# Token columns riding in the head sums of a backward chain, and key/value gradients moved into a weave

## The chip, the cores and the metric

The kernel runs on one core of one Trainium2 chip. The metric is the device time of one execution in microseconds (us). A span is the time from the first to the last instruction of a profiled execution. An instruction's place in the source is given as L and its line in the kernel before.

## What is computed

Forward and backward pass of a gated mix of two attention layers over 2048 tokens of 576 features, `g * a + (1 - g) * b`. Layer A is multi-query attention with 32 heads of 18. Layer B is attention with a recurrent memory; it is what the change is about:

```
for s in range(64):                                   # segments of 32 tokens
    h = concat([mem, x[32*s : 32*s + 32]])            # 8 memory rows, then 32 token rows
    q, k, v = (h @ W for W in (Wq, Wk, Wv))           # 32 heads of 128
    p = softmax(mask(q @ k.T * scale))                # token rows causal, memory columns free
    o = (p @ v) @ Wo
    mem, out[s] = o[:8], o[8:]
```

The outputs are the result and the gradients of all inputs and weights. The memory rows of a segment depend on those of the one before; in the backward pass their gradient runs through the 64 segments from last to first. All else of layer B can be done for many segments at once.

## The kernel before

**Stages.** They follow each other on the core: `prep` and `a_weights` (transposed copies of the inputs), `make_WoT`, `b_proj` (dense projections), the forward weave, `b_bulk` (token attention of layer B, forward and backward, but for some sums), the backward weave, `b_post` (the last token stage), `b_dw` (weight gradients) and `a_final`. From `make_WoT` to `b_post` instructions stand on each engine in the order in which the program writes them; every engine and every DMA queue works in that order and waits where an operand or a buffer isn't ready.

**A weave** (`weave`) is two generators that take turns: after each step of a chain (to its `yield`) comes one step of a sweep. The sweep is layer A's attention: `a_pass1` forward, `a_pass2` backward, 1024 pairs each. A step of `a_pass2` writes two 128 x 512 score tiles (`b_S`, one buffer), takes their exponential on ACT (`b_E`, L1652), makes two `b_dP` tiles, multiplies on DVE (`b_dS`, L1673) and adds four `b_acc` matmuls of the pair before. QD and SD (`b_QD`, `b_SD`) are loaded every fourth pair, two loads ahead. The chain has 16 steps for each of the 64 segments. In the backward weave the sweep gets 12 steps of lead and twice 10 extra ones at the start, in which `load_WT` brings the weights.

**The backward chain** (`b_chain_bwd`), by its steps: 1 to 3 project the memory's gradient (`dm`, 8 of 32 columns) to the heads (`proj_part`, L264); 4 transposes it (`mem_T`); 5 makes the score gradients `dS` of the memory rows and spreads them to blocks on POOL (`dSB`); 6, 7 and 8 make the gradients of v, q and k (`mem_grad`, for wi = 2, 0, 1), which ACT copies to `dT`, 256 columns for each wi: 8 groups u of 4 heads x 8 rows. `heads` multiplies them with the weights `WT`: for each half of the 576 features, wi and u, four matmuls side by side, one for each group of 8 heads g, each with all 32 columns of the group u on its 32 columns of the array. Of the 32 x 288 results of such a matmul a quarter is used, the head whose weights it has. `sums` picks it: matmuls in f32 with the selection matrix `selF`. `put_rows` (L272) writes the next `dm`. A segment's loads (`load`) are issued in step 8 on SP's queue, 14 and one transpose; small stores go through POOL's queue.

**The fifth slice.** 576 features are four slices of 128 and one of 64. The transposed inputs hold six slots (`NSL`): the fifth slice stands in two, one with its lower and one with its upper 64 rows zero, so that a matmul of it has 128 rows and takes the weights of one of two column halves that share 128 partitions (`W...t`). This holds in `b_proj`, in `b_chain_fwd` and in `b_chain_bwd` by `proj_part`.

**The forward chain** (`b_chain_fwd`) does the same for the memory rows; since its projections have 32 columns and only 8 memory rows, 24 token columns ride along (`put_ride`), and its `heads` (L384 on) multiply each head by itself, 32 x 4 matmuls of 144 columns.

**The last token stage** (`b_post`) has 16 token tiles with 8 groups of 4 heads, 128 group steps, pipelined over three stages: `st_KV` (L1100) adds to the gradients of k and v of the tile's tokens what comes from the tokens' own score gradients (loaded `y_ds`, `y_p`, `y_q`, `y_dO`) and what comes from the memory rows of its four segments (`y_sB` with the block-diagonal `y_qB` and `y_dOB`, cleared once on POOL at L1063); `st_T` transposes them on PE; `st_H` (L1129) multiplies dq, dk and dv with `WT` to the input's gradient, 24 matmuls of 288 columns (`y_pdx`), which goes to `dxB_dram`. dk and dv go to DRAM for `b_dw`.

Of the kernel before, what the change touches and what calls it, by code (L numbers as in the profile page):

```python
# [31 lines left out]
NSL = 6  # L32
# [8 lines left out]
class Kern:  # L41
# [52 lines left out]
    def setup_B_dram(self, dram):  # L94
        T, NSEG, NM, NTT = self.T, self.NSEG, self.NM, self.NTT
        t = lambda nm, sh, dt=BF16: dram.tile(sh, dt, name=nm)
        self.xT_dram = t("xT_dram", [NSL, P, T])
        self.dbT_dram = t("dbT_dram", [NSL, P, T])
# [6 lines left out]
        self.xtok = {w: t(w + "x_dram", [T, J]) for w in ("q", "k", "v", "o", "dO", "dq", "dk", "dv")}  # L105
# [9 lines left out]
        self.pq_dram = t("pq_dram", [NTT, 4, 8, 4, 16, P])  # L115
# [7 lines left out]
    def setup_B_consts(self, pool):  # L123
# [37 lines left out]
        sf = pool.tile([P, 8], F32, name="selF")  # L161
        nc.gpsimd.memset(sf[:], 0.0)
        for c in range(4):
            nc.gpsimd.affine_select(out=sn[:, c, :], in_=sn[:, c, :], compare_op=ALU.not_equal, fill=1.0,
                                    base=-32 * c, pattern=[[-1, 8]], channel_multiplier=1)
            nc.gpsimd.affine_select(out=sf[:], in_=sf[:], compare_op=ALU.not_equal, fill=1.0,
                                    base=-40 * c, pattern=[[-1, 8]], channel_multiplier=1)
        self.seln = sn
        self.selF = sf
# [10 lines left out]
        hm = pool.tile([P, 2, 8], BF16, name="halfmask")  # L180
        nc.gpsimd.memset(hm[:], 0.0)
        for j in range(2):
            nc.gpsimd.memset(hm[64 * j:64 * j + 64, j, :], 1.0)
        self.halfmask = hm
# [27 lines left out]
    def proj_load(self, items, n, sp):  # L212
        if n < len(items) and items[n] not in self.px:
            w, tt = items[n]
            t = sp.tile([P, NSL, P], BF16, name="p_x", bufs=4)
            src = self.dbT_dram if w == "dO" else self.xT_dram
            self.nc.sync.dma_start(t[:], src[:, :, tt * P:(tt + 1) * P].rearrange("k p t -> p k t"))
            for v in ("k", "v", "q") if w != "dO" else (w,):
                self.px[v, tt] = t
# [3 lines left out]
    def b_proj(self, items, n0, n1, sp, psum, extra):  # L223
        nc = self.nc
        due = []
        for n in range(n0, n1):
# [9 lines left out]
            for jc in range(8):  # L236
                pb = psum.tile([P, 512], F32, name="p_pb", bufs=8)
                for kt in range(4):
                    self.mm(pb[:], lhsT=xt[:, kt, :], rhs=Wt[0][:, kt, jc * 512:(jc + 1) * 512],
                            start=(kt == 0), stop=False)  # L240
                self.mm(pb[:], lhsT=xt[:, 4 + jc % 2, :], rhs=Wt[1][:, jc // 2, :], start=False, stop=True)
                self.evac(tok[:, jc * 512:(jc + 1) * 512], pb[:], use="vs"[jc % 2])
# [21 lines left out]
    def proj_part(self, pj, st, Wt, j, kts):  # L264
        for kt in kts:
            for c in range(4):
                lhsT, rhs = ((st[:, kt, :], Wt[0][:, kt, c * 1024 + j * 512:c * 1024 + (j + 1) * 512]) if kt < 4
                             else (st[:, 4 + j, :], Wt[1][:, c, :]))
                self.mm(pj[32 * c:32 * c + 32, :], lhsT=lhsT, rhs=rhs,
                        start=(kt == 0), stop=(kt == NKT - 1), tp=(0, 32 * c))  # L270

    def put_rows(self, t, pm):  # L272
        nc = self.nc
        nc.vector.tensor_copy(t[:, 0:4, 0:8], pm[:, 0:4, :])
        nc.vector.tensor_tensor(out=t[:, 4:6, 0:8], in0=pm[:, 4:5, :].to_broadcast([P, 2, 8]), in1=self.halfmask[:],
                                op=ALU.mult)
# [7 lines left out]
    def b_chain_fwd(self, keep, sp, psum):  # L284
        nc = self.nc
        NSEG = self.NSEG
        hm = [keep.tile([P, NSL, 32], BF16, name=f"hm{i}") for i in range(2)]
# [5 lines left out]
        for kt in range(NKT):  # L293
            for p0, n, r0 in d_rows(kt):
                for j in range(1 if kt < 4 else 2):
                    q0 = p0 + 64 * j
                    nc.gpsimd.dma_start(hm[0][q0:q0 + n, kt + j, 0:8], self.B_mem0[:, r0:r0 + n].rearrange("m d -> d m"))
# [7 lines left out]
        def load_stage(m):  # L305
            t0 = ride(4 * m)[0]
            n = min(96, self.T - t0)
            if n > 0:
                stage[m] = sp.tile([P, NSL, 96], BF16, name="c_rt", bufs=1)
# [9 lines left out]
        put_ride(0)  # L319
        nc.gpsimd.dma_start(self.otok_dram[:, D:NKT * P].rearrange("(n p) d -> p n d", p=P),  # L320
# [31 lines left out]
        for s in range(NSEG):  # L352
# [38 lines left out]
            if s:  # L391
                pm = psum.tile([P, NKT, 8], F32, name="c_pj", bufs=1)
                self.mm(pm[:, 0:4, :].rearrange("p k q -> p (k q)"), lhsT=hs[:],
                        rhs=self.seln[:].rearrange("p c q -> p (c q)"))
                for j in range(2):
                    self.mm(pm[64 * j:64 * j + 64, 4, :], lhsT=hx[:].rearrange("p g c -> p (g c)"), rhs=self.sel8[:],
                            tp=(0, 64 * j))
                self.put_rows(h_, pm)
            yield
            nc.gpsimd.tensor_copy(hist[:, :, s, :], h_[:, 0:NKT, 0:8])  # L400
# [8 lines left out]
            if s % 4 == 0:  # L409
                nc.gpsimd.dma_start(self.pq_dram[s // 4].rearrange("s q c w k -> (s q c) (w k)")  # L410
# [157 lines left out]
    def make_WoT(self, pool, psum):  # L568
        self.alloc_WoT(pool)
        W, Wt = self.WoT  # L570
        for kt in range(4):
            for hg in range(8):
                ptr = psum.tile([P, 640], BF16, name="w_ptr", bufs=4)
                for hl in range(4):
                    h = hg * 4 + hl
                    self.tr(ptr[:, hl * E:(hl + 1) * E], self.WoN[:, h, kt * P:kt * P + P], P)
                self.evac(W[:, kt, hg * 512:(hg + 1) * 512], ptr[:, 0:512])
            self.nc.sync.dma_start(self.st_WoT[kt], W[:, kt, :])
        for c in range(4):
            ptr = psum.tile([P, 640], BF16, name="w_ptr", bufs=4)  # L580
            for j in range(2):
                for hl in range(4):
                    h = 8 * c + 4 * j + hl
                    self.tr(ptr[64 * j:64 * j + 64, hl * E:(hl + 1) * E], self.WoN[:, h, 4 * P:D], P, tp=(0, 64 * j))
# [297 lines left out]
    def b_chain_bwd(self, keep, sp, psum):  # L882
        nc = self.nc
        NSEG = self.NSEG
        dm = [keep.tile([P, NSL, 32], BF16, name=f"dm{i}") for i in range(2)]
        self.load_WoT(keep)
        mrow = {w: keep.tile([P, 8, n * E], BF16, name=f"r_{w}") for w, n in (("q", 1), ("k", 1), ("dx", 2))}
        pads = {w: keep.tile([P, n, 8, 32], BF16, name=f"r_{w}pad") for w, n in (("p", 1), ("ds", 1), ("x", 2))}
        for t in dm + list(mrow.values()) + list(pads.values()):
# [3 lines left out]
        seln = f(self.seln[:])  # L893

        def load(s):
            L = {}
            L["vmT"] = sp.tile([P, HB, 8], BF16, name="r_vmT", bufs=2)
            nc.sync.dma_start(L["vmT"][:], self.mTd["v"][s])
            L["vxT"] = sp.tile([P, HB, 32], BF16, name="r_vxT", bufs=2)
# [3 lines left out]
            L["oT"] = sp.tile([P, 256], BF16, name="r_oT", bufs=2)  # L903
            nc.sync.dma_start(L["oT"][:], self.oTm_dram[s // 16][:, s % 16, :])
            L["kx"] = sp.tile([P, 8, E], BF16, name="r_kx", bufs=2)
            for c in range(4):
                nc.sync.dma_start(L["kx"][32 * c:32 * c + 32].rearrange("p u e -> p (u e)"),
                                  self.xtok["k"][s * 32:(s + 1) * 32, c * 1024:(c + 1) * 1024])
                nc.sync.dma_start(mrow["dx"][32 * c:32 * c + 8],
                                  self.dmx_dram[s * 8:s * 8 + 8, 8 * c:8 * c + 8].rearrange("m h w e -> m h (w e)"))  # L910
# [3 lines left out]

        def to_q(srcs, nm, eng):
            pad = pads[nm]
            for i, src in enumerate(srcs):
                eng.tensor_copy(pad[:, i, :, 0:8], u8(src))
# [9 lines left out]

        nxt = load(NSEG - 1)
        PqB = p_blocks(nxt["pT"])  # L930
        for s in reversed(range(NSEG)):
# [3 lines left out]
            nc.gpsimd.dma_start(self.dmT_dram[:, :, s, :], d_[:, 0:NKT, 0:8])  # L935
# [16 lines left out]
            for c in range(4):  # L952
                nc.gpsimd.dma_start(self.mtok["dO"][s * 8:(s + 1) * 8, c * 1024:(c + 1) * 1024], self.m_rows(dOm, c))
            yield
# [10 lines left out]
            for rg in range(2):  # L965
                for c in range(4):
                    self.mm(pd[32 * c:32 * c + 32, rg, :], lhsT=self.negones[:, 0:32], rhs=prod[:, :, c, :],
                            start=False, stop=True, tp=(0, 32 * c))
            dS = sp.tile([P, 2, 64], BF16, name="r_dS", bufs=1)
# [4 lines left out]
            dT = sp.tile([P, 3, 8, 32], BF16, name="r_dT", bufs=1)  # L974
            hs = sp.tile([P, D], F32, name="r_hs", bufs=1)
            ph = {}

            units = iter([(wi, hf, u) for hf in range(2) for wi in (2, 0, 1) for u in range(8)])

            def heads(n):  # L980
                for _ in range(n):
                    wi, hf, u = next(units)
                    if hf not in ph:
                        ph[hf] = psum.tile([P, 288], F32, name="r_pj", bufs=1)
                    for g in range(4):
                        self.mm(ph[hf][32 * g:32 * g + 32, :], lhsT=dT[:, wi, u, :],
                                rhs=self.WT[wi][:, 8 * g + u, 288 * hf:288 * hf + 288],
# [946 lines left out]
```

## Time and profile before

| | us |
|---|---|
| median of 3 runs | 6115.3 |
| the runs | 6114.51, 6115.3, 6123.61 |
| the profiled execution | 6121.41 |
| its span | 6119.6 |

| engine | busy us | share of the span |
|---|---|---|
| PE | 5639.4 | 92% |
| DVE | 3758.4 | 61% |
| ACT | 3423.1 | 56% |
| POOL | 2163.7 | 35% |

PE is TensorE's matmuls, PEld its weight loads, DVE VectorE, ACT ScalarE, POOL GpSimd, SP the engine that only issues DMAs; SPq is its queue. A line of the timeline has the start in us from the span's start, the time in us from the first of merged instructions to the end of the last, engine, line, operation, `out<-in`, the stationary operand's rows and columns joined by `*`, the moving operand's partitions and elements, and a count; in brackets stands the idle time before it and what ended it. Matmuls are pipelined: the time of a single one (0.39 for 512 columns) is longer than what it adds to a row of them (0.215), so the distance between two starts tells what work costs. L76 and L81 are the helpers that issue all matmuls and most transposes, so that they are told by the names of their tiles.

### The profile page before, as it was taken

How to read it: one execution, taken by the hardware profiler on the slowest of the kernel's cores; microseconds unless marked ns; L12 is line 12 of the kernel's file. 1: busy time of each engine (PE TensorE's matmuls, PEld its weight loads, DVE VectorE, ACT ScalarE, POOL GpSimd, SP SyncE). 2: the span in 40 equal slices, each digit the busy share in tenths (PEclk: the TensorE clock that was granted, in tenths of full speed). 3: DMA queues.
4: the chain of work that ended last, by engine and by line, in shares of the span. 5: the costliest groups of instructions: out<-in, count | busy, mean ns of one | idle time of the engine just before them, and what ended most of it. 6: DMA issues, size and time to landing. Idle time of an engine off the chain costs nothing.

```text
span 6119.6 us, 211593 instructions
## 1 busy us (share of the span) xinstructions
PE 5639.4 (92%) x90477; PEld 3286.1 (54%) x90477; DVE 3758.4 (61%) x7114; ACT 3423.1 (56%) x4842; POOL 2163.7 (35%) x3896
## 2 busy tenths in 40 slices
PE   6899999999999979998879999999998999899999
PEld 4443444444444438777535555555554777675444
DVE  4326888888888866666668888888886111111112
ACT  3325788788787866555557777777775222111101
POOL 4003555545555544444323333333333111112213
PEclk9999999999999989999889999999999999999999
DMA  4644665656565459999853434444443999896663
GB/s 152 221 157 134 134 139 133 139 138 140 133 138 114 107 143 251 252 243 249 246 144 109 108 108 109 109 108 110 109 109 96 239 250 249 236 274 202 209 187 113
DMA packets 1117299, 1000.59 MB, mean 164 GB/s; under 512 B 687353, under 2 KB 942722, under 8 KB 1106722
## 3 DMA queue, kind: packets, MB, share of 16 engines
q1 hardware_dynamic: 1009090, 724.23, 46.0%
q0 software_dynamic: 107264, 262.81, 14.4%
q8 instruction: 709, 11.62, 0.8%
q14 instruction: 236, 1.93, 0.1%
HBM read 551.36 MB, written 386.08 MB: 153 GB/s over the span
## 4 chain that ended last, share of the span: by engine, by line
PE 62%; ACT 14%; DMA 7%; issue 2%; SPq 2%; POOL 1%; DVE 0%; POOLq 0%; DVEq 0%; ACTq 0%
ACT b_E L1652 11%; PE w_acc L76 10%; PE a_acc L76 7%; PE b_S L76 6%; PE c_pj L76 5%; PE y_pdx L76 5%; PE a_S L76 5%; PE r_pj L76 4%; PE c_x L76 3%; DMA dsx_dram<-x_dS 3%; ACT a_E L1515 3%; PE r_x L76 3%; PE x_tr L81 2%; PE b_acc L76 2%; PE y_pk L76 2%
## 5 line engine op out<-in xcount | busy, mean ns | idle before, releaser
L1543 DVE TENSOR_TENSOR a_W<-a_dP,a_E 128x512 bf16<-128x512 f32 x2048 | 1313.0, 685 | 281.7 <-ACT c_k L73 60.6
L1673 DVE TENSOR_TENSOR b_dS<-b_dP,b_E 128x512 bf16<-128x512 f32 x2048 | 1312.9, 682 | 254.0 <-issue 132.8
L1652 ACT ACTIVATE b_E<-b_S 128x1024 bf16<-128x1024 f32 x1024 | 1048.8, 1024 | 423.3 <-PE b_dP L76 326.1
L1515 ACT ACTIVATE a_E<-a_S 128x1024 bf16<-128x1024 f32 x1024 | 1049.2, 1025 | 290.0 <-PE a_dP L76 278.9
L76 PE MATMUL b_S<-b_KV,b_QD 32*128 32x512 bf16 x2048 | 405.9, 386 | 161.4 <-ACT b_E L1652 116.4
L76 PE MATMUL r_pj<-WT,r_dT 128*32 128x288 bf16 x12288 | 494.6, 289 | 1.1 <-ACT r_hs L990 1.1
L76 PE MATMUL w_acc<-w_d,w_h 128*128 128x512 bf16 (+1 forms) x2400 | 473.8, 379 | 0.0
L76 PE MATMUL a_S<-a_QD,l_KV 32*128 32x512 bf16 x2048 | 399.3, 383 | 33.3 <-ACT a_E L1515 18.7
L76 PE MATMUL a_acc<-a_W,l_WK 128*32 128x512 bf16 x4096 | 429.2, 390 | 0.3 <-DVE a_W L1543 0.2
L76 PE MATMUL b_acc<-b_dS,b_SD 128*32 128x512 bf16 x2048 | 423.8, 395 | 0.6 <-DMA b_SD<-sd_dram 0.4
L76 PE MATMUL a_acc<-a_E,l_VK 128*32 128x512 bf16 x4096 | 415.1, 381 | 5.6 <-issue 1.1
L76 PE MATMUL b_acc<-b_E,b_SD 128*32 128x512 bf16 x2048 | 408.8, 396 | 0.0
L76 PE MATMUL a_dP<-a_QD,l_KV 32*128 32x512 bf16 x2048 | 407.3, 385 | 0.0
L76 PE MATMUL b_dP<-b_KV,b_QD 32*128 32x512 bf16 x2048 | 403.9, 391 | 0.0
L1125 DVE COPY y_T<-y_pt 128x512 bf16<-128x512 bf16 x256 | 96.9, 419 | 460.9 <-PE y_pt L81 442.8
L76 PEld LDWEIGHTS <-r_dT 128*32 128x32 bf16 x12288 | 334.6, 97 | 80.0 <-issue 2.3
L76 PEld LDWEIGHTS <-w_h 128*128 128x128 bf16 (+1 forms) x2688 | 229.8, 100 | 258.4 <-issue 6.6
L76 PEld LDWEIGHTS <-b_QD 32*128 32x128 bf16 x4096 | 166.5, 91 | 357.5 <-issue 313.2
L76 PEld LDWEIGHTS <-hm 128*32 128x32 bf16 x7680 | 195.9, 97 | 207.2 <-POOL hm L316 10.7
L1111 ACT CAST y_tdk<-y_pk 128x512 bf16<-128x512 f32 x128 | 75.1, 587 | 380.1 <-PE y_pk L76 214.8
L76 PE MATMUL y_pdx<-WT,y_T 128*128 128x288 bf16 x2048 | 272.9, 287 | 0.0
L725 POOL TENSOR_TENSOR x_P<-x_E,x_r 128x512 bf16<-128x512 bf16 x128 | 133.3, 1041 | 388.3 <-DVE x_r L722 298.2
(444 smaller groups left out, 11603.2 us busy)
## 6 DMA issues: line engine op xcount, KB each, us to landing
b_QD<-qd_dram SPq DMA_DIRECT2D x256, 128.0 KB
b_SD<-sd_dram SPq DMA_DIRECT2D x256, 128.0 KB
dOx_dram<-p_tok SPq DMA_DIRECT2D x16, 1024.0 KB
c_vx<-vx_dram SPq DMA_DIRECT2D x256, 64.0 KB
krow_dram<-c_k POOLq DMA_DIRECT2D x64, 256.0 KB, 2.9
qrow_dram<-c_q POOLq DMA_DIRECT2D x64, 256.0 KB, 3.9
vrow_dram<-c_v POOLq DMA_DIRECT2D x64, 256.0 KB, 3.3
x_q<-qx_dram SPq DMA_DIRECT2D x32, 512.0 KB
```

Of the source, the lines that this page charges most:

```text
L76: return self.nc.tensor.matmul(out, lhsT, rhs, start=start, stop=stop, tile_position=tp, skip_group_check=True)
L81: return self.nc.tensor.transpose(out, in_, self.identB[b:b + nrows, b:b + nrows], tile_position=tp)
L725: nc.gpsimd.tensor_tensor(out=o[:, r, :], in0=Et[:, :, lo:lo + n], in1=rl[:].unsqueeze(2).to_broadcast([P, 4, n]), op=ALU.mult)
L1111: nc.scalar.copy(d[w][:, r, :], pk[:])
L1125: nc.vector.tensor_copy(T_[t][w][:], pt[:])
L1515: nc.scalar.activation(E_[n][:], S.pop(n)[:], ACT.Exp, scale=SCALEA)
L1543: nc.vector.tensor_tensor(out=W_[n][:, i, :], in0=dP[i][:], in1=E_[n][:, i, :], op=ALU.mult)
L1652: nc.scalar.activation(E_[n][:], S.pop(n)[:], ACT.Exp, scale=SCALEA)
L1673: nc.vector.tensor_tensor(out=D_[n][:, i, :], in0=dP[i][:], in1=E_[n][:, i, :], op=ALU.mult)
```

## The change

1. **Riding columns.** `dT` is one kept tile with 32 columns for each of the 32 heads and three gradients. Columns 24 to 31 are the memory rows, which ACT writes as before (and POOL copies to `dTc` for the store); columns 0 to 23 are 24 tokens' dq, dk and dv, which three DMA transposes a segment (`load_dT`) bring from DRAM for 55 of the 64 segments: the last 1320 tokens. `heads` has 96 units instead of 48, each one head and gradient, with four matmuls of 144 columns that cover the 576 features; nothing of a result is thrown away. Two DVE copies, one bf16 matmul and two small ones (`row_sums`, as in the forward chain) take the place of the f32 sums, and the sums' rows 0 to 23 go to `dxr_dram`, from which four DRAM copies in the last stage fill the rows of `dxB_dram`.
2. **Key and value gradients in the weave.** `st_KV`'s work for tiles 15 down to 5 is done in the backward chain, 176 units of four heads and one of dk and dv, four a segment in 44 segments: `kv_mm` in steps 4, 10, 13 and 16, `kv_out` (an ACT copy and a store on POOL, with one buffer) in steps 5, 11, 14 and 16. The memory rows' part is four matmuls of 32 rows instead of one block-diagonal one of 128.
3. **The last stage** has 6 tiles, tokens 0 to 767, and the 32-row form of the sums as well; the block-diagonal buffers and their clearing go.
4. **The fifth slice** has one slot: its matmuls have 64 rows, at row 0 or 64 of the array. `put_rows` is one copy. The columns of `db` and of Wo's transpose are permuted to groups of 144, with four small POOL copies in `make_WoT` and 16 in `prep`.
5. **Buffers.** Several of the chain's loads have one buffer instead of two; `b_KV` is loaded in four parts with two buffers.

The core of the diff:

```diff
@@ proj_part
-                lhsT, rhs = ((st[:, kt, :], Wt[0][:, kt, c * 1024 + j * 512:c * 1024 + (j + 1) * 512]) if kt < 4
-                             else (st[:, 4 + j, :], Wt[1][:, c, :]))
+                r = slice(64 * j, 64 * j + 64)
+                lhsT, rhs, r0 = ((st[:, kt, :], Wt[0][:, kt, c * 1024 + j * 512:c * 1024 + (j + 1) * 512], 0) if kt < 4
+                                 else (st[r, 4, :], Wt[1][r, c, :], 64 * j))
                 self.mm(pj[32 * c:32 * c + 32, :], lhsT=lhsT, rhs=rhs,
-                        start=(kt == 0), stop=(kt == NKT - 1), tp=(0, 32 * c))
+                        start=(kt == 0), stop=(kt == NKT - 1), tp=(r0, 32 * c))
+
+    def row_sums(self, pm, hs, hx, sel, sel8):
+        self.mm(pm[:, 0:4, :].rearrange("p k q -> p (k q)"), lhsT=hs[:, 0:P], rhs=sel[:].rearrange("p c q -> p (c q)"))
+        for j in range(2):
+            self.mm(pm[64 * j:64 * j + 64, 4, :], lhsT=hx[:].rearrange("p g c -> p (g c)"), rhs=sel8[:], tp=(0, 64 * j))
@@ b_chain_bwd
+        def load_dT(s, wi):
+            if 0 <= s < NSEG - KR:
+                t0 = T - RIDE * (NSEG - KR - s)
+                nc.sync.dma_start_transpose(dT[:, wi], self.xtok[("dq", "dk", "dv")[wi]][t0:t0 + 32, :])
...
+        def kv_load(n):
...
+            if w == 0:
+                nc.sync.dma_start(kvS[rg].rearrange("p x i k -> p (x i k)"),
+                                  self.pq_dram[tt, g // 2].rearrange("s q h x i k -> (s q) h (x i k)")[:, g % 2, :])
+                for j, x in enumerate(("dO", "q")):
+                    nc.sync.dma_start(kvR[rg, j].rearrange("p i e -> p (i e)"),
+                                      self.mtok[x][tt * 32:tt * 32 + 32, 512 * g:512 * g + 512])
+            a = sp.tile([P, 4, P], BF16, name="r_ks", bufs=2)
+            nc.sync.dma_start(a[:], (self.dsx_dram if w else self.px_dram)[tt][:, 4 * g:4 * g + 4, :])
+            b = sp.tile([P, 4, P], BF16, name="r_kr", bufs=2)
...
+        def kv_mm(n, tag):
...
+            for i in range(4):
+                self.mm(pk[:, i, :], lhsT=kvS[rg, w, i, :], rhs=kvR[rg, w, i, :], start=True, stop=False, tp=(rg.start, 0))
+            for i in range(4):
+                self.mm(pk[:, i, :], lhsT=a[:, i, :], rhs=b[:, i, :], start=False, stop=True)
+            kvo[n] = pk
+            kv_load(n + 2)
+
+        def kv_out(n):
...
+            o = sp.tile([P, 4, P], BF16, name="r_kvo", bufs=1)
+            nc.scalar.copy(o[:], kvo.pop(n)[:])
+            nc.gpsimd.dma_start(self.xtok["dk" if w else "dv"][tt * P:(tt + 1) * P, 512 * g:512 * g + 512],
+                                o[:].rearrange("p h e -> p (h e)"))
...
-                        self.mm(ph[hf][32 * g:32 * g + 32, :], lhsT=dT[:, wi, u, :],
-                                rhs=self.WT[wi][:, 8 * g + u, 288 * hf:288 * hf + 288],
-                                start=(wi == 2 and u == 0), stop=(wi == 1 and u == 7), tp=(0, 32 * g))
+                        self.mm(ph[32 * g:32 * g + 32, 0:GD], lhsT=dT[:, wi, 8 * c + u, :],
+                                rhs=self.WT[wi][:, 8 * c + u, GD * g:GD * g + GD],
+                                start=(wi == 2 and u + c == 0), stop=(wi == 1 and u + c == 10), tp=(0, 32 * g))
...
-                nc.scalar.copy(dT[:, wi], pg[:])
+                dst = dT[:, wi].rearrange("p (c u) t -> p u c t", u=8)[:, :, :, RIDE:32]
+                nc.scalar.copy(dst, pg[:].rearrange("p u (c t) -> p u c t", t=8))
+                nc.gpsimd.tensor_copy(dTc[:, wi], dst)
...
+            kv_mm(n0 + 1, "r_x")
+            heads(8)
...
+            kv_out(n0 + 1)
+            heads(13)
+            load_dT(s - 1, 2)
             yield
+            heads(13)
+            yield
+            kv_mm(n0 + 2, "r_x")
+            heads(8)
+            yield
+            kv_out(n0 + 2)
+            heads(13)
+            load_dT(s - 1, 0)
...
+            heads(12)
+            hs = sp.tile([P, GD], BF16, name="r_hs", bufs=1)
+            nc.vector.tensor_copy(hs[:], ph[:, 0:GD])
+            hx = sp.tile([P, 4, 16], BF16, name="r_hx", bufs=1)
...
+            self.row_sums(pm, hs, hx, self.sel24, self.sel8b)
+            kv_mm(n0 + 3, "r_x")
             dn = dm[1 - s % 2]
             self.put_rows(dn, pm)
+            nc.gpsimd.dma_start(self.dxr_dram[s], hs[:])
+            load_dT(s - 1, 1)
+            kv_out(n0 + 3)
             yield
@@ b_post
+        T0 = self.T - RIDE * (self.NSEG - KR)
+        NTT = (T0 + P - 1) // P
```

## The prediction

> **What bounds the kernel now.** I read the page's engine table first (PE busy 92% of the span, far ahead of DVE with 61% and ACT with 56%), then the busy time by stage, because the change touches three stages and each may have a limit of its own. The three rows are the forward weave, the backward weave and the last token stage:
>
> ```profile
> core 0: us, PE busy (x) PEld busy (x) DVE busy (x) ACT busy (x) POOL busy (x), PEclk, DMA share, GB/s
> 515.00:2245.00 1730.00, 1683.94 (x35479) 770.53 (x35479) 1436.73 (x2613) 1374.50 (x1723) 873.29 (x1789) 1.00 0.56 129
> ...
> 3010.00:4728.00 1718.00, 1535.79 (x32069) 858.30 (x32069) 1434.06 (x2562) 1232.84 (x1540) 603.49 (x1044) 0.97 0.43 115
> 4728.00:5320.00 592.00, 557.59 (x5416) 445.54 (x5416) 101.18 (x273) 147.66 (x272) 86.98 (x155) 0.97 0.93 236
> ```
>
> The last stage runs its 16 x 8 group steps on PE alone, back to back, beside DMAs that are 93% busy. In the timeline of PE, from one y_dOB sum to the next:
>
> ```profile
> 4773.85 0.38 PE L76 MATMUL y_pk<-y_dOB,y_sB 128*128 128x512 bf16 x1
> 4774.07 0.39 PE L76 MATMUL y_pk<-y_dO,y_p 128*128 128x128 bf16 x4
> ...
> 4774.74 1.14 PE L76 MATMUL y_pdx<-WT,y_dq 128*128 128x288 bf16 x8
> 4775.72 2.12 PE L76 MATMUL y_pdx<-WT,y_T 128*128 128x288 bf16 x16
> 4777.68 0.38 PE L76 MATMUL y_pk<-y_qB,y_sB 128*128 128x512 bf16 x1
> 4777.89 0.39 PE L76 MATMUL y_pk<-y_q,y_ds 128*128 128x128 bf16 x4
> 4778.11 0.38 PE L76 MATMUL y_pk<-y_dOB,y_sB 128*128 128x512 bf16 x1
> ```
>
> A step takes 4.26 us; with its DMA waits the stretch 4755.5 to 5316, which holds 128 of them, gives 560.5/128 = 4.38.
>
> The weaves differ. In the backward one, PE and ACT form a loop: a score matmul needs the one b_S buffer that the exponential before it reads. The timelines of PE and, below it, of ACT:
>
> ```profile
> 3906.06 0.91 PE L76 MATMUL r_pj<-WT,r_dT 128*32 128x288 bf16 x24
> 3907.06 0.39 PE L76 MATMUL b_S<-b_KV,b_QD 32*128 32x512 bf16 x2
> ...
> 3907.39 0.39 PE L76 MATMUL b_acc<-b_E,b_SD 128*32 128x512 bf16 x2
> 3907.61 0.91 PE L76 MATMUL r_pj<-WT,r_dT 128*32 128x288 bf16 x24
> 3908.61 0.39 PE L76 MATMUL b_S<-b_KV,b_QD 32*128 32x512 bf16 x2
> ```
>
> ```profile
> 3907.53 1.02 ACT L1652 ACTIVATE b_E<-b_S 128x1024 bf16<-128x1024 f32 x1 [0.53 <-PE b_dP L76]
> ```
>
> 1.02 of exponential and 0.53 until the next scores: **no step is shorter than 1.55**. A step is longer only where PE has more to do. A backward segment (16 steps) takes 25.6 (pd sums at 3899.8 and 3925.4), 0.8 over 16 x 1.55: 0.2 in the first memory gradient's step, 0.1 each in two others, 0.4 where four f32 sums follow 24 head matmuls (3911.77 to 3913.71).
>
> One price more: changing the tile shape on PE. a_final has a 64-row matmul among 128-row ones (forms 128*128 and 64*128 of one tile); three full ones and it should take 4 x 0.215 = 0.86 and take 1.06:
>
> ```profile
> 6056.89 1.13 PE L76 MATMUL f_big<-f_wqT,f_T 128*128 128x512 bf16 x4
> 6057.95 0.39 PE L76 MATMUL f_big<-f_wkvT,w_h 128*128 128x512 bf16 x1
> ```
>
> So entering and leaving another shape costs 0.10 each. The same 0.10 stands between b_S and b_acc above (0.32 for 0.22 of streaming).
>
> **The change, part by part** (against the profiled execution, 6121.4 with a span of 6119.6; the median of the runs is 6115.3, 6 lower).
>
> *Last stage, 16 tiles to 6.* 128 steps become 48. In each, the two 512-wide sums become twice four 32-row matmuls of 128 columns: the same streaming, but four more changes of shape, 0.40. 48 x (4.38 + 0.40) = 229, so 560 - 229 = 331 goes. The memsets of the block-diagonal buffers, which hold the stage's first loads from 4726.1 to 4733.2, go too: 7. Ends: 128 - 48 = 80 steps at 4.26 with nothing added to the rest and the 7, 348; 5.0 a step because DMAs stay late, 320. **I take -338.** Loads per step stay equal, the 256-byte ones of the block-diagonal buffers go, so PE sets the step.
>
> *Forward weave.* The fifth slice of a projection was 128 rows, half of them zero, in the shape of its neighbours; it becomes 64 rows. Six per segment. Four of a segment's steps hold such a slice among 16 projection matmuls and have no slack; between two scores such a step takes 1.73, with no idle time of PE:
>
> ```profile
> 1520.48 0.39 PE L76 MATMUL a_S<-a_QD,l_KV 32*128 32x512 bf16 x2
> ...
> 1522.21 0.39 PE L76 MATMUL a_S<-a_QD,l_KV 32*128 32x512 bf16 x2
> ```
>
> Each gets an entry and an exit: 4 x 0.20. The fifth step (v, half 0) has about 0.15 of slack: 0.06. The sixth ends in a change that is there anyway and fits below 1.55. 0.86 x 64 segments = **+55**. The shape 64*32 occurs in no row; the ends are 0 (no drain) and 11 changes x 0.10 x 64 = 70. I take the row above, the only 64-row one. The one copy less in put_rows is hidden: PE is busy with transposes at that point. In the dense projection before it, two 64-row matmuls run side by side and save 0.215, less 0.20 for their shape: nothing.
>
> *Small ones at nothing:* 16 tail copies on POOL in prep (0.23 each, as xtail's) and four in make_WoT lie beside PE's waits for DMA (21.6 and 14.3 before 240 us); uncovered, some 8. The head sums now need all columns of WT, so the first ones wait for its fourth DMA, issued at 3055.2 with 16 to 33 to land, and start at 3080 already now: 0 to 8, once. Four DRAM copies on POOL in the last stage land long before a_final reads them.
>
> *Backward weave, what stays equal.* 192 head matmuls of 288 columns become 384 of 144. The forward weave has that form:
>
> ```profile
> 1515.73 0.86 PE L76 MATMUL c_pj<-WoN,c_oT 128*8 128x144 bf16 x44
> ```
>
> 0.86 less the last one's 0.23 is ten quadruples (four run side by side): 0.063 each, 16 ns a matmul, 96 x 0.063 = 6.0 a segment. Now it is 0.91 - 0.29 over five, 48 x 0.124 = 6.0: equal. The Trainium skill, "TensorE: Matmul & The Clock Gate", section "Wait — 56ns, not 53.3ns?", speaks against it: start to start never drops below about 25 ns however few the columns. By that, 384 matmuls would take 9.6, 3.6 more a segment, 230 more over the weave, and the sum would be about 6130. The row of 44 has four column tiles at once and shows 16; I follow the row.
>
> *Backward weave, what is added.* 176 key/value units, four a segment in 44 of 64 segments: each four 32-row and four full matmuls of 128 columns (8 x 0.056, as y_pk's four take 0.22) with two changes of shape, 0.65; an ACT copy of 0.59 (as y_tdk); a store; two to five loads. Over a segment:
> - two units share a step with 32 head matmuls: 0.31 + 0.22 + 0.65 + 0.50 + 2 x 0.10 = 1.88, which is 0.33 over 1.55, twice: +0.66. One shares the transposes' step (where PE idles 0.53 now): +0.04. One is in the last step with the sums: +0.15, the DVE copies ahead of them (0.28 and 0.21) included.
> - the 13-unit head steps take 13 x 0.063 = 0.82 against 0.74 for 24 now, under the loop: 0. The f32 sums go: -0.40.
> - three ACT copies of 0.59 stand in the 0.53 that ACT waits: +0.15 with their hand-over.
> - on POOL, one store issue (0.54) now stands ahead of dSB, and copies of dT (0.43, as c_oh) ahead of dSqB; dSB has 0.6 of slack and the third gradient none: +0.1.
> - the stores share one buffer. The third copy of a segment ends 2.6 before the fourth may start; the store between them takes 0.05 plus 3.0 (dTm_dram's median from issue to landing). ACT waits about +0.6, and the loop with it. Ends: 0, and 5.2 to land (dkx_dram in the last stage), 2.6.
>
> Together +1.3 in 44 segments and -0.3 in 20: +57 - 6 = 51. SP: its issue goes from about 13 to 20 of 26 us a segment (three transposes of 1.27 and 14 loads of 0.35 more, three dx loads fewer); QD and SD, loaded five steps ahead, stand behind them. I add 8 for single late ones. **+59**; ends -26 (only the 0.40 saved, all else hidden) and +215 (all matmuls and the copies' 0.05 on the path, 2.6 of store wait).
>
> *Sum:* 6121.4 - 338 + 55 + 59 = **5897**.
>
> **The rivals.**
> - *The single store buffer holds the fourth unit* for 2.6, 2.0 over what I took: 2.0 x 44 = 88 more, 5985. For: DMA share, by the packets added, goes from 0.43 to about 0.8, and the last stage's stores land in 5.2 to 6.3 at 0.93. Against: small stores of the weave land in 2.2 to 3.4.
> - *64-row slices don't drain the 32-column shape:* 5897 - 55 = 5842.
> - *It doesn't shrink as it says:* the last stage, with a DMA share of 0.93, is held by its loads; at 5.6 a step, 48 x 0.8 = 39 more, 5936. For: y_dO loads on the chain. Against: PE idles only about 14 in 560.
> - *Slower:* QD comes late. At 3093.75 SP issues b_QD behind a burst, and PE waits 9.7 for it, with the DMAs full of WT. If transposes of 1024 packets ahead of it in the one SP queue do this in each of 55 segments, 55 x 9.7 = 534: 6430. It decides from (6115 - 5897)/55 = 4.0 a segment. Against: 1.3 of issue each, and five steps (8 us) of lead.
>
> **How the numbers follow.** Forecast 0.58; store buffer 0.18; no drain 0.11; loads hold the last stage 0.08; late QD 0.05, of which 0.04 beyond the point that decides. A difference under 0.2% (12 us) could not be told from none. The time is 5897; the range 5810 to 6000 takes in no drain with a smaller weave, and the store buffer with 20 of late loads. Faster 0.95, same 0.01, slower 0.04.
>
> **What would show it.** Right: y_pdx matmuls fall from 3072 to 1152 and the last stage to about 235; forward steps of 1.73 become 1.93; a backward segment with units takes about 26.9, with 1.88 in its tenth and thirteenth step and ACT waiting for the store of r_kvo in its last. Wrong: b_S waiting for DMA in most segments, or r_pj matmuls 25 ns apart.

## The result, and the profile after

| | before | after |
|---|---|---|
| median, us | 6118.1 (4 runs) | 6085.4 (4 runs, 6077.8 to 6092.5) |
| ratio, 95% interval | 1 | 0.9946, 0.9928 to 0.9963 |
| the profiled execution | 6121.4 | 6084.0 (span 6082.2) |

The change makes the kernel half a per cent faster, not 3.6% as forecast, and the time lies far outside the range. The busy time by stage of the changed kernel, which answers to the three rows shown of before:

```profile
core 0: us, PE busy (x) PEld busy (x) DVE busy (x) ACT busy (x) POOL busy (x), PEclk, DMA share, GB/s
515.00:2300.00 1785.00, 1749.88 (x35483) 738.35 (x35483) 1432.64 (x2550) 1389.46 (x1723) 871.96 (x1793) 1.00 0.53 124
3060.00:5035.00 1975.00, 1727.67 (x45189) 976.86 (x45189) 1480.68 (x2627) 1276.42 (x1588) 808.65 (x1479) 0.94 0.70 165
5035.00:5285.00 250.00, 232.99 (x2344) 179.54 (x2344) 40.59 (x112) 60.12 (x102) 33.66 (x58) 0.95 0.79 214
```

By their first and last matmuls (lines of the changed kernel are two to some ninety further down: L78 issues matmuls, L1743 is the exponential, L1766 the products, L999 and L1000 are the unit's copy and store, L946 and L948 the padding copy and the transpose of `to_q`):

| stage | before | after | difference | forecast |
|---|---|---|---|---|
| forward weave | 1738.7 | 1795.1 | +56.4 | +55 |
| backward weave | 1713.2 | 1969.1 | +255.9 | +59 |
| last token stage | 580.5 | 241.8 | -338.7 | -338 |
| all else | | | -11.0 | 0 |

The 11 of all else are four differences of 2 to 4 ahead of, between and behind these stages; they were not looked into.

The last stage does what was worked out: a group step is 4.70 in the timeline of PE, from one sum of the k gradients to the next (its four 32-row matmuls cost 0.33 with their changes of shape):

```profile
5104.19 0.39 PE L78 MATMUL y_pk<-y_mR,y_sB 32*128 32x128 bf16 x4
5104.52 0.40 PE L78 MATMUL y_pk<-y_q,y_ds 128*128 128x128 bf16 x4
...
5106.83 2.12 PE L78 MATMUL y_pdx<-WT,y_T 128*128 128x288 bf16 x16
5108.89 0.39 PE L78 MATMUL y_pk<-y_mR,y_sB 32*128 32x128 bf16 x4
```

**One term of the sum is wrong, by 197.** The row of the backward weave says where to look: its PE is busy 0.87 of the time (0.89 before), its clock is 0.94 instead of 0.97, and it issues 45189 matmuls instead of 32069. By segments: 25.6 before; with units 31.2 on average (forecast 26.9); in the last segments, which have no units, 26.7 (forecast 25.3). By steps, from one score matmul to the next, the mean over 42 segments and over 13 without units:

| step | 5 | 6 | 7 | 8 | 9 | 10 | 11 | 12 | 13 | 14 | 15 | 16 | 1 | 2 | 3 | 4 |
|---|---|---|---|---|---|---|---|---|---|---|---|---|---|---|---|---|
| before | 1.55 | 1.56 | 1.76 | 1.65 | 1.55 | 1.56 | 1.55 | 1.61 | 1.95 | 1.55 | 1.55 | 1.55 | 1.55 | 1.55 | 1.58 | 1.56 |
| after | 1.67 | 1.56 | 2.08 | 1.93 | 1.70 | 1.97 | 1.59 | 1.83 | 2.09 | 1.79 | 2.57 | 2.99 | 2.37 | 1.81 | 1.57 | 1.63 |
| after, no units | 1.57 | 1.55 | 1.77 | 1.65 | 1.70 | 1.58 | 1.55 | 1.97 | 1.62 | 1.89 | 1.83 | 1.70 | 1.67 | 1.55 | 1.55 | 1.55 |

The table begins with step 5, in which a segment's first unit is copied and stored, and steps 1 to 4 stand last. Steps 10 and 13 have a median of 1.93, where 1.88 was forecast. The loss sits elsewhere: in 15, 16 and 1, in 7 and 8, and spread over 9 to 15, in segments without units too. One such place in the changed kernel, first its timeline of POOL, then of ACT, DVE and PE:

```profile
4040.38 2.42 POOL L1095 DMA_DIRECT2D pq_dram<-r_xq  x4 [1.84 <-DVE r_xq L948]
4042.74 0.63 POOL L1000 DMA_DIRECT2D dkx_dram<-r_kvo  x1
4048.33 0.56 POOL L1000 DMA_DIRECT2D dvx_dram<-r_kvo  x1 [4.95 <-ACT r_kvo L999]
4048.88 0.25 POOL L946 COPY r_ppad<-r_pT 128x64 bf16<-128x64 bf16 x1
```

```profile
4040.98 0.58 ACT L999 CAST r_kvo<-r_x 128x512 bf16<-128x512 f32 x1
...
4045.63 1.02 ACT L1743 ACTIVATE b_E<-b_S 128x1024 bf16<-128x1024 f32 x1 [1.44 <-PE b_dP L78]
4047.44 0.59 ACT L999 CAST r_kvo<-r_x 128x512 bf16<-128x512 f32 x1 [0.79 <-DMA dkx_dram<-r_kvo]
4047.93 1.03 ACT L1743 ACTIVATE b_E<-b_S 128x1024 bf16<-128x1024 f32 x1
```

```profile
4045.67 1.29 DVE L1766 TENSOR_TENSOR b_dS<-b_dP,b_E 128x512 bf16<-128x512 f32 x2 [1.18 <-issue]
4049.16 0.45 DVE L948 STREAM_TRANSPOSE r_pq<-r_ppad 128x256 bf16<-128x256 bf16 x1 [2.20 <-POOL r_ppad L946]
```

```profile
4049.01 0.39 PE L78 MATMUL b_S<-b_KV,b_QD 32*128 32x512 bf16 x2 [0.82 <-ACT b_E L1743]
4049.97 0.64 PE L78 MATMUL b_dP<-b_KV,b_QD 32*128 32x512 bf16 x2 [0.57 <-issue]
```

Read it from the top. The second unit's store is ready at 4041.6 (ACT's copy), but POOL is still issuing four stores of `xq`, so it is issued at 4042.74. The third unit's copy needs the same buffer and waits on ACT until that store has landed, 4047.44; behind it stands an exponential. The third store is on POOL at 4048.33, behind it the padding copy of the next segment's p, and DVE, in order, has waited 2.20 for that copy with products behind it. PE is idle twice.

### The profile page after: what moved, and what is told of

The parts are those of the page before. It is cut to its first block, busy times and chain, and to the rows that moved or that the text cites. A ratio compares the mean times of both kernels' runs of the same rounds, so it can differ in the third digit from the quotient of the medians.

```text
span 6082.2 us, 232056 instructions
## 1 busy us (share of the span) xinstructions
PE 5560.4 (91%) x100314; PEld 3084.6 (51%) x100525; DVE 3740.7 (62%) x6956; ACT 3393.5 (56%) x4720; POOL 2316.7 (38%) x4261
## 3 DMA queue, kind: packets, MB, share of 16 engines
q14 instruction: 241, 1.97, 0.1%
## 5 line engine op out<-in xcount | busy, mean ns | idle before, releaser
L1766 DVE TENSOR_TENSOR b_dS<-b_dP,b_E 128x512 bf16<-128x512 f32 x2048 | 1312.6, 683 | 347.6 <-issue 217.1
L1743 ACT ACTIVATE b_E<-b_S 128x1024 bf16<-128x1024 f32 x1024 | 1049.2, 1025 | 494.8 <-PE b_dP L78 375.4
L78 PE MATMUL r_pj<-WT,r_dT 128*32 128x144 bf16 x24576 | 525.8, 229 | 62.4 <-issue 59.6
L78 PE MATMUL b_S<-b_KV,b_QD 32*128 32x512 bf16 x2048 | 416.8, 398 | 123.5 <-ACT b_E L1743 98.2
L78 PEld LDWEIGHTS <-r_dT 128*32 128x32 bf16 x24576 | 437.5, 98 | 128.3 <-issue 80.0
L78 PE MATMUL w_acc<-w_d,w_h 128*128 128x512 bf16 (+1 forms) x2352 | 471.0, 379 | 2.5
L78 PE MATMUL b_dP<-b_KV,b_QD 32*128 32x512 bf16 x2048 | 433.9, 401 | 31.3 <-DVE b_dS L1766 28.0
L78 PE MATMUL b_acc<-b_dS,b_SD 128*32 128x512 bf16 x2048 | 452.0, 407 | 2.1 <-issue 0.9
L78 PE MATMUL a_acc<-a_W,l_WK 128*32 128x512 bf16 x4096 | 429.7, 390 | 0.3 <-DVE a_W L1628 0.2
L78 PE MATMUL b_acc<-b_E,b_SD 128*32 128x512 bf16 x2048 | 422.4, 409 | 2.6 <-issue 2.6
L78 PE MATMUL a_S<-a_QD,l_KV 32*128 32x512 bf16 x2048 | 398.4, 384 | 26.5 <-ACT a_E L1600 17.3
L78 PE MATMUL a_acc<-a_E,l_VK 128*32 128x512 bf16 x4096 | 415.2, 381 | 4.8 <-issue 0.3
L78 PE MATMUL a_dP<-a_QD,l_KV 32*128 32x512 bf16 x2048 | 403.4, 385 | 0.0
L78 PEld LDWEIGHTS <-w_h 128*128 128x128 bf16 (+1 forms) x2688 | 229.9, 100 | 258.4 <-issue 6.6
L78 PEld LDWEIGHTS <-hm 128*32 128x32 bf16 (+1 forms) x7680 | 177.9, 94 | 344.2 <-issue 221.8
L78 PEld LDWEIGHTS <-b_QD 32*128 32x128 bf16 x4096 | 148.7, 91 | 289.8 <-issue 203.2
L78 PEld LDWEIGHTS <-b_SD 128*32 128x32 bf16 x4096 | 117.1, 93 | 323.6 <-issue 313.6
L75 ACT CAST w_o<-w_acc 128x512 bf16<-128x512 f32 x54 | 31.6, 586 | 384.3 <-PE w_acc L78 364.5
L73 DVE CAST w_o<-w_acc 128x512 bf16<-128x512 f32 x54 | 37.4, 692 | 333.4 <-PE w_acc L78 306.1
```

Source lines behind the costliest of these rows:

```text
L73: nc.vector.tensor_copy(out, in_)
L75: nc.scalar.copy(out, in_)
L78: return self.nc.tensor.matmul(out, lhsT, rhs, start=start, stop=stop, tile_position=tp, skip_group_check=True)
L1743: nc.scalar.activation(E_[n][:], S.pop(n)[:], ACT.Exp, scale=SCALEA)
L1766: nc.vector.tensor_tensor(out=D_[n][:, i, :], in0=dP[i][:], in1=E_[n][:, i, :], op=ALU.mult)
```

## The experiments

Two theories came out of these lines: B, the one store buffer, and Q, the order of the work in POOL's queue. A third, F, came out of the segments without units: PE's instructions, which are fetched by DMA, come too slowly. Each run is compared with the kernel before on the same chip; the weave is that of the profiled execution.

| kernel | time, us | ratio to before, 95% interval | backward weave | segment with units | without |
|---|---|---|---|---|---|
| the changed kernel | 6085.4 | 0.9946, 0.9928 to 0.9963 | 1969.1 | 31.2 | 26.7 |
| two store buffers | 6020.5 | 0.9831, 0.9817 to 0.9846 | 1897.4 | 29.5 | 26.7 |
| early block of p | 6067.4 | 0.9919, 0.9887 to 0.9950 | 1947.4 | 30.6 | 26.9 |
| both | 6008.4 | 0.9811, 0.9795 to 0.9827 | 1885.7 | 29.1 | 27.0 |
| wide head sums | 6081.4 | 0.9928, 0.9913 to 0.9943 | 1949.1 | 31.3 | 25.5 |
| both + late first store | 5995.3 | 0.9792, 0.9776 to 0.9808 | 1867.5 | 28.7 | 27.4 |
| both + wide | 5892.0 | 0.9618, 0.9603 to 0.9632 | 1763.0 | 27.0 | 25.5 |
| both + late + wide | 5871.1 | 0.9591, 0.9574 to 0.9609 | 1749.0 | 26.7 | 25.5 |
| both + late, padded forward | 5940.1 | 0.9703, 0.9689 to 0.9718 | 1874.5 | 28.8 | 27.1 |
| the same, 192 whole head sums | 5904.2 | 0.9638, 0.9625 to 0.9651 | 1837.3 | 28.2 | 26.3 |
| the same, riding sum moved | 5839.7 | 0.9538, 0.9525 to 0.9551 | 1770.6 | 27.0 | 25.7 |

### Two store buffers

```diff
-            o = sp.tile([P, 4, P], BF16, name="r_kvo", bufs=1)
+            o = sp.tile([P, 4, P], BF16, name="r_kvo", bufs=2)
```

> The changed kernel (6085) with r_kvo in two buffers instead of one; nothing else. Its backward weave takes 1969 where 1772 was forecast. Theory Q (queue): in step 14 the store of a key/value unit is issued on POOL ahead of the padding copy of the next segment's p; DVE, which takes its work in order, holds the transpose of that copy (DVE r_pq waits for POOL r_ppad 99.0 in 42 segments, 2.3 each) and behind it the products that free PE. The wait of ACT for the store of the one buffer (42.0 + 17.3 in 43 segments, 1.4 each) is only the first part of that chain: it goes here, about half of the 2.3 stays. Weave 40 to 80 shorter, time 6005 to 6045. Theory B (buffer): the one buffer is the cause of all of it: weave 130 to 200 shorter, 5885 to 5955. Theory F (instruction fetch): PE's instructions per us rose, and it waits for them ('issue' before r_pj, 40.2 in all): 0 to 20 shorter, 6065 to 6085.

The weave is 72 shorter, as theory Q has it. The waits of the changed kernel and then of this one, in 3250 to 4580 (total us, times, longest):

```profile
DVE r_pq L948 <- POOL r_ppad L946: 99.0, 42, 4.1
...
ACT r_kvo L999 <- PE r_x L78: 50.1, 30, 2.4
ACT r_kvo L999 <- DMA dkx_dram<-r_kvo: 42.0, 36, 2.6
...
PE r_pj L78 <- issue: 40.2, 49, 2.6
...
ACT r_kvo L999 <- DMA dvx_dram<-r_kvo: 17.3, 9, 2.4
```

```profile
DVE r_pq L948 <- POOL r_ppad L946: 56.1, 43, 1.3
...
ACT r_kvo L999 <- PE r_x L78: 36.4, 44, 2.1
```

No copy waits for a store any more, and DVE's wait for the padding copy is nearly halved, for the store ahead of it leaves earlier.

### The block of p ahead of the store

```diff
+            if s:
+                PqB = p_blocks(nxt["pT"])
             kv_out(n0 + 2)
             heads(13)
             load_dT(s - 1, 0)
-            if s:
-                PqB = p_blocks(nxt["pT"])
```

> The changed kernel with the block of the next segment's p (padding copy on POOL, transpose on DVE, expansion on POOL) issued at the head of step 14, ahead of the unit's copy and store; still one buffer of r_kvo. Theory Q: the 2.3 a segment of DVE's r_pq goes; ACT's wait for the buffer (1.4 a segment) stays and still delays one exponential: weave 80 to 130 shorter, 5955 to 6005. Theory B: 0 to 20 shorter, 6065 to 6085. Theory F: the same 0 to 20.

Only 22 shorter, close to the 0 to 20 of theories B and F: theory Q, which gave this place the larger part, is wrong in its weights. DVE's wait is gone, but ACT's for the one buffer has grown from 59.3 to 101.3. The waits of this kernel:

```profile
ACT r_kvo L999 <- DMA dvx_dram<-r_kvo: 53.7, 33, 3.0
ACT r_kvo L999 <- DMA dkx_dram<-r_kvo: 47.6, 39, 2.3
```

Of the 99 that DVE no longer waits, 42 came back as waits of ACT for the buffer. Both together:

> Both: two buffers of r_kvo and the block of p ahead of the store. Theory Q: weave 130 to 190 shorter, 5895 to 5955, with segments of 27 to 28. Theory B: as with two buffers alone, within 10. Theory F: a rest of 1 to 1.5 a segment stays in all 64 segments, also in the 16 without units (26.5 now against 25.3 forecast), 60 to 100 in all, so the time does not go under 5950.

6008, 83 off the weave, as theory F's bound of 5950 allows and theory Q's 5955 does not. One by one the two edits gave 72 and 22, so they overlap by little. The segments without units stay at 27.0: neither the buffer nor POOL's order is their cause.

### Half as many head matmuls

The DMA queues of the changed kernel in 3250 to 4580 hold one that carries instructions (packets, MB, share of the DMA engines):

```profile
q8 instruction: 240, 3.93, 1.2%
```

It brings 240 packets while PE runs 61418 matmuls and weight loads: 256 for each packet, so I take it for PE's. A head step issues 52 head matmuls and 8 of the sweep and as many weight loads, 120 in 1.55, so it needs a packet every 3.3. By the trace's DMA records, packets in the segments without units start 4.6 apart (median; the closest 3.4), and PE stops in the middle of a row of equal matmuls that wait for nothing. The changed kernel's timeline of PE there:

```profile
4710.89 0.39 PE L78 MATMUL b_S<-b_KV,b_QD 32*128 32x512 bf16 x2
...
4711.45 0.61 PE L78 MATMUL r_pj<-WT,r_dT 128*32 128x144 bf16 x27
4712.55 0.28 PE L78 MATMUL r_pj<-WT,r_dT 128*32 128x144 bf16 x5 [0.49 <-issue]
4712.76 0.39 PE L78 MATMUL b_S<-b_KV,b_QD 32*128 32x512 bf16 x2
```

It goes on at 4712.55, 1.35 after a packet landed (4711.20 by the records); the next two stops, at 4716.84 and 4720.86, end 1.31 and 1.36 after one. Before the change a head step had 24 + 8 matmuls, and in the same 1330 us no r_pj matmul waited so. That it is the packets, and not the weight loads or the matmuls themselves, shows in when PE goes on: of the changed kernel's 49 stops ahead of an r_pj matmul in 3250 to 4580 that end without a releaser (40.2 in all), 46 (37.6) end 1.25 to 1.65 after a packet landed; by chance, with packets 5.5 apart on average, it would be some 4. The test keeps the columns and halves the matmuls:

```diff
                     wi, u, c = next(units)
+                    if c % 2:
+                        continue
                     for g in range(4):
-                        self.mm(ph[32 * g:32 * g + 32, 0:GD], lhsT=dT[:, wi, 8 * c + u, :],
-                                rhs=self.WT[wi][:, 8 * c + u, GD * g:GD * g + GD],
+                        self.mm(ph[32 * g:32 * g + 32, 0:288], lhsT=dT[:, wi, 8 * c + u, :],
+                                rhs=self.WT[wi][:, 8 * c + u, GD * (g % 3):GD * (g % 3) + 288],
...
```

> The changed kernel with the head sums of the weave in half as many matmuls of twice as many columns: 192 of 288 instead of 384 of 144 a segment, the same columns in all. Part of the computation is changed: each second unit of the head sums is left out, and the others sum 288 columns of the weight, of which 144 are of a wrong group. One buffer, and the store ahead of the block, as in the changed kernel. Theory F: the gaps of PE that end 1.25 to 1.65 after one of its instruction fetches landed (58.8 in the 1330 us with units, 17 in the 16 segments behind them), and the slower clock behind them, go: weave 70 to 150 shorter, segments without units at 25.3 to 25.6. Theories Q and B: 0 to 20 shorter, and the segments without units stay at 26.5.

Half a miss. The segments without units fall to 25.5, the forecast's 25.3 nearly. But those with units don't move: their steps 15 and 16 grow, 2.57 and 2.99 to 2.82 and 3.33. The second unit's store is issued when POOL has done with `xq` and lands 4.3 after that (median), whatever PE does meanwhile; what PE gains ahead of it, it waits longer.

So the same edit was made where that wait is gone:

> The kernel with two buffers and the early block of p (6008), with the head sums in half as many matmuls of twice as many columns (part of the computation is changed: each second unit of the head sums is left out, the others sum 288 columns of which 144 are of a wrong group). In the changed kernel the wide form took the segments without units from 26.7 to 25.4, but not those with units (31.2), where the chain of the store came last. Theory F (with that chain gone, instruction fetch is what is left): segments with units from 29.1 to 27.3 to 27.8, those without to 25.4, weave 90 to 110 shorter, 5895 to 5920. Rival D (what is left in segments with units is the load of DMA and queues): only the 20 segments without units gain, 25 to 30 shorter, 5975 to 5985.

123 off the weave where it had been 20: theory F, with segments of 27.0 and 25.5; the weave gains 13 more than the 90 to 110 written, and the median, 5892, is 3 under the range. In 3250 to 4580 no r_pj matmul stops without a releaser any more. Rival D falls. The 1150 us from 3250 on, with the columns of the busy time by stage, first of the changed kernel and then of this one:

```profile
3250.00:4400.00 1150.00, 1038.60 (x26520) 583.73 (x26516) 862.65 (x1520) 762.82 (x968) 482.54 (x890) 0.95 0.74 174
```

```profile
3250.00:4400.00 1150.00, 1101.85 (x22323) 588.70 (x22323) 986.78 (x1745) 872.73 (x1111) 554.50 (x1024) 0.99 0.86 198
```

The DMAs are busier in the faster kernel, 0.86 against 0.74.

### The first store behind dSB

```diff
-            kv_out(n0)
+            kv_out(n0, True)
...
             self.expand(dSB[:], dS[:].rearrange("p a (u q) -> p (a u) q", q=8), 16)
+            kv_store()
...
```

With `True`, `kv_out` only makes the copy; `kv_store` issues the store.

> The kernel with two buffers and the early block of p (6008, weave 1886), and in step 5 the store of the first unit is issued on POOL behind the expansion of dSB instead of ahead of it. Theory S (the store's issue of 0.58 makes dSB late, so that PE and DVE run late in steps 7 and 8, 2.07 and 1.92 on average against 1.77 and 1.65 in segments without units): 0.57 x 44 = 25 shorter, 5975 to 5990. Rival: it is ACT's copy of 0.58 in step 5, which stays: 0 to 5 shorter.

Steps 7 and 8 fall from 2.07 and 1.92 to 1.82 and 1.70, 0.47 a segment where theory S has 0.57, 18 off the weave; the median, 5995, is 13 lower and 5 above the range given. All three edits:

> All three: two buffers and the early block, the late first store, and the wide head sums (the same part of the computation changed). If the store chain, the first store's place and instruction fetch are the whole of the difference, segments with units take 26.9, as forecast, the weave 1765 to 1785 and the run 5875 to 5900. Each 10 above that is cause not yet found.

5871, 4 under what was written, with segments of 26.7 (forecast 26.9). Nothing of the 197 is left over; the weave, 1749, is even 23 under the forecast of 1772, of which 8 are the forecast's term for late QD.

### The fifth slice of the forward chain

The forward chain gets back its two half-zero slots, and only it (`pad`; the slots and their filling are left out here):

```diff
...
+                                 else (st[:, 4 + j, :], Wt[1][:, c, :], 0) if pad
                                  else (st[r, 4, :], Wt[1][r, c, :], 64 * j))
...
```

> Two buffers, the early block and the late first store (whole computation), and in the forward chain alone the fifth slice of a projection back in 128 rows, half of them zero, in the shape of its neighbours (a masked product on DVE and three copies on POOL a segment in place of one each). Theory: the forward weave's 56 came from the changes of tile shape alone: the forward weave goes from 1795 back to 1739 to 1745, the time to 5920 to 5935. Rival: it came from something else in the forward chain, such as the layout of the weights: 0 to 10 shorter than the kernel with the late first store.

The forward weave goes from 1798.8 to 1737.5; the time is 55 lower than with the late first store and, like that, some 5 above what was written. A step with the slice, in the changed kernel and then in this one:

```profile
1521.20 0.39 PE L78 MATMUL c_pj<-Wk,hm 128*32 128x512 bf16 x4
1521.52 0.40 PE L78 MATMUL c_pj<-Wkt,hm 64*32 64x512 bf16 x4
1521.85 0.62 PE L78 MATMUL c_x<-Wk,hm 128*32 128x512 bf16 x8
```

```profile
1519.52 0.39 PE L78 MATMUL c_pj<-Wk,hm 128*32 128x512 bf16 x4
1519.73 0.39 PE L78 MATMUL c_pj<-Wkt,hm 128*32 128x512 bf16 x4
1519.95 0.61 PE L78 MATMUL c_x<-Wk,hm 128*32 128x512 bf16 x8
```

From start to start 0.32 and 0.33 against 0.21 and 0.22: 0.11 for each change of shape, with the same matmuls at twice the rows.

### Fewer instructions, with the whole computation

Wide sums that leave nothing out need the four groups' results added up:

```diff
+                    hf, wi, u = next(units)
...
-                        self.mm(ph[32 * g:32 * g + 32, 0:GD], lhsT=dT[:, wi, 8 * c + u, :],
-                                rhs=self.WT[wi][:, 8 * c + u, GD * g:GD * g + GD],
+                        self.mm(ph[hf][32 * g:32 * g + 32, :], lhsT=dT[:, wi, 8 * g + u, :],
+                                rhs=self.WT[wi][:, 8 * g + u, 288 * hf:288 * hf + 288],
...
+            for kt in range(4):
+                self.mm(pm[:, kt, :], lhsT=hs[:, GD * kt:GD * kt + P], rhs=self.sel8b[:])
...
+            for g in range(4):
+                self.mm(pb[32 * g:32 * g + 32, 64:64 + GD], lhsT=self.sel32[:], rhs=hs[:, GD * g:GD * g + GD], tp=(0, 32 * g))
```

> The whole computation with fewer PE instructions: on the kernel with two buffers, early block, late first store and padded forward slices (5940), the head sums of the weave as 192 matmuls of 288 columns: column group g sums the 8 heads 8g to 8g+7 over all columns, in two halves, and the four groups are added by six small matmuls (memory rows) and four of 144 columns (riding rows) in the last step. Theory F: the fetch of instructions goes as in the runs that left units out (124 shorter there), less 10 to 40 for the added copies on DVE and ACT and the matmuls of the last step: 5830 to 5860. Rival: those runs were shorter because half the head units were left out, or the added sums on the path from one segment to the next take it back: 5900 to 5960.

5904: inside the rival's range. The instructions do arrive (steps 9 to 15 are as in the run with three edits, to 0.1, and no r_pj matmul stops without a releaser), but the last step takes 2.91. Its timeline of PE:

```profile
3965.55 0.20 PE L78 MATMUL r_pj<-sel8b,r_ht 128*64 128x8 bf16 x2
3966.66 0.25 PE L78 MATMUL r_pj<-r_hs,sel 128*32 128x144 bf16 x4 [0.91 <-DVE dm L299]
```

A wait of my own making: the riding rows' sum wrote the same tile that DVE had still to read. Moved:

> The kernel before it (5904, whole computation, 192 matmuls of 288 columns) with the sum of the riding rows taken out of the last step: there its four matmuls wrote the tile that DVE's dm still had to read, PE waited 0.91 a segment for it and the last step took 2.91 (2.25 in segments without units) against 1.55. It now goes into r_x in the ninth step of the next segment, where ACT has no copy. Theory F, with the added wait as the reason why the run before missed its range: the last step falls to 1.6 to 1.9, 44 x 1.1 + 20 x 0.6 = 60 shorter, 5835 to 5865. Rival: the last step is long because of the longer copies on DVE ahead of the sums (0.45 + 0.18): 0 to 20 shorter.

5839.7, within what was written, with a last step of 1.75, and **4.6% faster than before (0.9538, 0.9525 to 0.9551)**, with the whole computation. The backward weave takes 1770.6; the forecast for it was 1713.2 + 59 = 1772. That the two agree is in part chance: this kernel has copies and sums that the forecast one has not.

## Why the prediction was wrong, by its steps

- **Last stage, -338:** -338.7. The trade of a 512-wide sum for four 32-row matmuls costs what the one row of a_final said.
- **Forward weave, +55:** +56.4, and the padded form takes it back. "Forward steps of 1.73 become 1.93": they became 1.96.
- **"The 13-unit head steps take 13 x 0.063 = 0.82 against 0.74 for 24 now, under the loop: 0"** is the step that failed. The 16 ns a matmul hold (the 27 above take 0.61, less 0.23 for the last one, over six quadruples: 0.063), and the 25 ns that were weighed against it do not hold here, with four column tiles side by side. But doubling the head matmuls doubled their instructions, and the supply of these was not in the sum. With the store's chain gone it costs 118 to 123, the slower clock behind PE's stops included (both against both + wide 1885.7 - 1763.0; with the late store 1867.5 - 1749.0). The row of before that was near, 44 matmuls in a row in the forward weave, shows the rate of one step; the backward chain has seven such steps in a row.
- **"The stores share one buffer ... about +0.6"** was mis-sized. The second buffer alone gives 72 / 44 = 1.6 a segment. The rival gave the same mechanism 2.0 more than forecast, 88 in all, but both looked at the wrong pair: the fourth copy behind the third store. In most segments it is the third behind the second (36 waits of ACT in 3250 to 4580, 42.0, against 9 and 17.3 for the fourth behind the third). The second store stands on POOL behind four stores of `xq` (2.42), and lands 4.7 after its issue (median), not 3.
- **"On POOL, one store issue (0.54) now stands ahead of dSB ...: +0.1"** was 0.4: the late first store gives 18 / 44. The early block of p, which the working did not have at all, gives 12 beside two buffers. These two sizes are rough: a backward weave with the same program took 1867.5 in one kernel (late first store) and 1874.5 in another (padded forward).
- **Late QD, 8, and the rival on the other side:** no b_S matmul in 3250 to 4580 waits for a DMA, and the weight loads that wait for b_QD come to 0.8 in all. Nothing.

In the order in which they were undone: 72 + 12 + 18 + 118 = 220, against the 197 that were missing; the last of these runs is the one 23 under the forecast. The order matters for what is put down to each: the wide sums give 20 when they are undone first and 123 when undone behind the store's chain.

Part of each of these is the clock. Step 1 has 16 projection matmuls and no new work, yet it takes 2.37 in the changed kernel and 1.66 with all three edits. In 20 of 42 segments of the changed kernel its granted clock is 0.50 to 0.60, and it takes 2.45 to 2.80 without a stop of PE; in the other 22 it takes 1.71 at the median, and up to 2.8 where PE also stops in it. In 3250 to 4580 the granted clock is 0.50 for 133 us in the changed kernel, at no time in the kernel before, and for 17 us with all three edits. So the stops cost more than their own time; how much of the 197 this is stays open, for no run holds the clock fixed.

## What to carry to other kernels

When a matmul is cut into narrower ones of the same total, count the instructions per us over the whole stretch, beside the columns: a row of the trace that shows the rate in one burst does not show that the supply of instructions lasts. When a step adds a store on an in-order queue, write down the queue for a whole period, what stands ahead of the store and what behind it; the wait here was made some steps ahead of the place where it showed. And undo suspected costs together as well as singly: the wide sums gave 20 while the store's chain ended the same steps, and 123 without it.

## What the runs showed of the hardware that was not expected

*Instruction supply.* In head steps that need a packet of 256 instructions every 3.3 us, packets started 4.6 apart (median of the segments without units, the closest 3.4), and PE ran dry. With the wide sums they started 6.4 to 6.9 apart (medians of the five kernels in 3250 to 4580), PE was not short of them, and a higher DMA share (0.86) did no harm. What sets the time of a packet was not tried.

*The clock.* A stop of PE of two or three us is often paid again behind it: in 3250 to 4580 of the changed kernel the granted clock falls to 0.50 25 times, for 3.4 or 6.8 us each. The changed kernel, stretches of one place (columns as in the first table of the profile):

```profile
4074.00:4080.00 6.00, 5.64 (x208) 3.70 (x202) 3.50 (x6) 2.66 (x3) 1.32 (x3) 1.00 1.17 197
4080.00:4083.00 3.00, 0.51 (x11) 0.19 (x4) 1.05 (x3) 2.24 (x3) 1.26 (x3) 1.00 1.09 158
4083.00:4090.00 7.00, 6.98 (x56) 2.21 (x59) 4.44 (x10) 2.79 (x4) 2.16 (x4) 0.52 0.59 170
4091.00:4096.00 5.00, 4.92 (x131) 2.47 (x129) 4.52 (x9) 4.54 (x7) 2.08 (x4) 1.00 0.43 109
```

PE works 0.51 of 3.00, and for the next 7.00, in which it is busy 6.98, the granted clock is 0.52; then it is 1.00 again. The Trainium skill, "TensorE: Matmul & The Clock Gate", section "Part 1: The HAM clock gate (the "warmup" mystery)", has the array drop to half its clock after an idle window of about 3.4 us. Here it dropped after stops of 1.67 and 0.84 with matmuls between them, so the row shows that less than a whole window without work is enough.
